# Attention and a top-2 mixture of experts on one core: another order of the slots by hand

## The chip, the cores and the metric

The program runs on one core of one Trainium2 chip. The metric is the time of one execution on the device in microseconds. Five runs of the kernel before gave 513.17, 511.36, 506.5, 507.58 and 507.99 us: a median of 507.99 (506.5 to 513.17).

## The reference

Blockwise causal attention (8 batches, 8 heads, 576 positions, head size 64, blocks of 64) is followed by a router that picks two of eight experts for each of the 4608 tokens, and by the experts themselves, two layers each.

```python
scores = scale * np.matmul(q, k.transpose(0, 1, 3, 2))
mask = block_i >= block_j
scores = np.where(mask, scores, -1000000000.0)
attn = np.exp(scores - max); attn = attn / attn.sum
x = np.matmul(attn, v)            # as (4608, 512): heads side by side
...
logits = x @ w_gate
noise_scale = np.log1p(np.exp(x @ w_noise))
noisy_logits = logits + noise_scale * noise
top2 = np.argpartition(-noisy_logits, 2, axis=1)[:, :2]
top2_w = softmax over the two
for e in range(E):
    h = np.maximum(x[mask] @ w1[e], 0.0)
    out[mask] += top2_w[mask, k, None] * (h @ w2[e])
```

## The kernel before, in words

**Attention.** The eight batches are worked in four groups of two batches (`NG = 4`). q and k of a group come in five chunks (0 to 4) through a ring of eight raw buffers each (`load_qk`, line 200), on GpSimd's queue. `transpose_qk` turns a chunk on TensorE (L250; the half chunks "4A" and "4B" on L252) into a PSUM tile of a pool with two buffers, and copies it into `qT` or `kT`: q on VectorE (L255), k on ScalarE (L262), k of chunk 1 on VectorE (L260); after chunk 0 a small VectorE copy (L265) follows. Both lie in one tile, `hq`, that the experts use again later. Chunk c holds blocks 16c to 16c+15 of a group's heads, so head h needs blocks 9h to 9h+8.

A group is 26 units (`UG`): two sets of four heads, three pieces of scores a head and one unit for the last block. A unit is TensorE matmuls (L292, L303) into one of two PSUM tiles `sc`, and one exp on ScalarE (L295, L306) into `esc`; the last unit of a set also zeroes parts of `esc` on VectorE (L309). `av_tile` multiplies `esc` by v (L333, L344) into one of two PSUM buffers "av" and normalises on VectorE (reciprocal L348, multiply L349) into the rows `xr`; the first tile of a group also zeroes the tail of `xr` (L322). v is loaded by `load_v` (L207) into one of two tiles, one for even and one for odd groups.

**Router.** `x_transpose` (L363, copy L364 on VectorE) turns a group's rows, and the generator `router` does the rest in 16 steps: steps 0 to 2 are the logits matmuls (L376) with their activations (L380 to L382), step 8 is two matmuls that count rows per expert (L420, L421), and the others are VectorE work on small tiles; the last sets `slots`. Then `scatter` (L484) writes 36 row tiles per pair of groups into `xd[half]` by indirect DMAs from GpSimd's queue, 18 a group; each also waits for the last but one pacing activation (`pace[-2]`). Groups 0 and 1 make half 0, groups 2 and 3 half 1.

**Experts.** Sixteen blocks (`SEQ`: experts 0, 1, 2 of half 0, the same of half 1, then in turn) each do `layer1` (L559, activation L562) and `layer2` (L571); layer 1's first part of the next block stands ahead of layer 2. `load_x` (L504) loads a block's rows by a transposing DMA from SyncE's queue, once all 36 scatters of its half have landed; `load_rec` (L511) loads the rows' records under the same condition, and `read_rec` turns them into row numbers and weights. Layer 2 writes `ysb` (four buffers, L576), stored by SyncE (L577); for a token's second expert the first one's rows are gathered (L598), added (L580) and the output row is written (L582), both indirect DMAs on GpSimd's queue. In block order, the load of block 3's x (expert 0 of half 1) stands behind the stores of block 1 and `load_rec(1)` on SyncE's queue. `load_w` (L227) loads weights on GpSimd's queue in four parts per expert: experts 0 and 1 into a pool `wE` with two buffers of its own, expert 2 into `wM`, which lies where the raw chunks of q and k lay and is opened, with the x tiles, after the last of these are turned.

**What sets the order.** Nothing is scheduled by a program: each engine runs its instructions in the order in which they are written. After each score unit u, `run(u)` issues what was put into slot u by `at(slot, fn, ...)`, in the order in which it was put there. Slots 0 to 103 are the attention units, 104 and 105 stand alone, and from 106 on each slot follows one step (`layer1` or `layer2` tile) of the experts. A queue runs its DMAs in the order of issue, and a DMA on GpSimd's or SyncE's queue also waits for the one eight places before it on that queue.

Of the kernel before, what the change touches and what calls it, by code (L numbers as in the profile page):

```python
# [19 lines left out]
def kernel(  # L20
# [23 lines left out]
    TG = 9  # L44
# [19 lines left out]
    UG = 2 * UN  # L64
# [32 lines left out]
    wE = main.enter_context(tc.tile_pool(name="wE", bufs=2))  # L97
# [112 lines left out]
    def v_loads(g):  # L210
        return [(load_v, g, idx) + r for idx in range(TG) for r in token_rows(g, idx)]
# [257 lines left out]

    RSTEPS = 16  # L470
    rgen = {}

    def router_step(g):
        if g not in rgen:
            rgen[g] = router(g)
        next(rgen[g])

    scat = [[] for _ in range(NH)]
    zfill = [[] for _ in range(NH)]
# [134 lines left out]
    todo = {}  # L614

    def at(slot, fn, *args):
        todo.setdefault(slot, []).append((fn, args))

    def run(slot):
        for fn, args in todo.pop(slot, ()):  # L620
            fn(*args)

    def after(ins, slot):
# [75 lines left out]
    for g in range(NG):  # L699
        s0 = g * UG  # L700
        last = g == NG - 1

        for nm, ch, i in (("q", 1, 0), ("k", 1, 3), ("k", 2, 5), ("q", 2, 7), ("k", "4A", 8), ("q", "4A", 9),
                          ("q", 3, 15), ("k", 3, 16)):
            at(s0 + i, transpose_qk, g, nm, ch)
        if not last:
            for nm, ch, i in (("q", 0, 14), ("k", 0, 17), ("q", "4B", 24), ("k", "4B", 24)):
                at(s0 + i, transpose_qk, g + 1, nm, ch)
            for i, (fn, *a) in enumerate(v_loads(g + 1)):
                at(s0 + 10 + i, fn, *a)  # L710
            at(s0 + 18, load_qk, g + 1, (2,))
            at(s0 + 20, load_qk, g + 1, (3,))
        if g + 2 < NG:
            for i, ch in ((21, 4), (22, 0), (24, 1)):
                at(s0 + i, load_qk, g + 2, (ch,))
        for i, a in enumerate((16, 16, 17, 18, 19, 19, 20, 21)):
            at(s0 + a, av_tile, g, 0, i)
        for i in range(2):
            at(s0 + 22 + i, av_tile, g, 0, 8, i)
        r0 = s0 + UG  # L720
        if not last:
            avs = (1, 2, 2, 4, 5, 5, 6, 7, 9, 10)
            xts_ = (6, 8, 11, 11, 12)
        if g < 2:
            rsl = (13, 13, 14, 17, 18, 19, 20, 21, 23, 24, 25, 26, 27, 28, 30, 31)
            r1 = 31
        elif g == 2:
            rsl = (13, 13, 14, 16, 17, 17, 18, 19, 21, 22, 22, 23, 23, 24, 24, 25)
            r1 = 26
        else:  # L730
            avs, xts_ = (0, 0, 1, 1, 2, 2, 3, 3, 4, 4), range(2, 7)
            rsl = (7, 7, 7, 8, 9, 9, 10, 11, 12, 13, 13, 14, 14, 15, 15, 16)
            r1 = 16
        for i in range(8):
            at(r0 + avs[i], av_tile, g, 1, i)
        for i in range(2):
            at(r0 + avs[8 + i], av_tile, g, 1, 8, i)
        for j in range(5):
            at(r0 + xts_[j], x_transpose, g, j)
        for j in range(RSTEPS):  # L740
            at(r0 + rsl[j], router_step, g)
        for j in range(2 * TG):
            at(r0 + r1 + (4 * j // 5 if last else j), scatter, g, j)
    at(4, setup_consts)
    at(3, sort_nz, 0)
    at(5, transpose_nz, 0)
    at(5, spread_nz, 0, 0)
    at(7, spread_nz, 0, 1)
    at(9, sort_nz, 1)
    at(12, transpose_nz, 1)  # L750
    at(12, spread_nz, 1, 0)
    at(13, spread_nz, 1, 1)
    at(UG + 4, clear_x, 0, UG + 3)
    at(2 * UG + 4, clear_x, 1, 2 * UG + 3)
    for k in range(4):
        at(2 * UG + k, load_w, wE, 0, k)
        at(3 * UG + 7 + 2 * k, load_w, wE, 1, k)
    for u in range(NG * UG):
        score_unit(*divmod(u, UG))
        run(u)  # L760
        if u == 3 * UG + 19:
            raws_up.close()
            ffn["x"] = raws_up.enter_context(tc.tile_pool(name="xgp", bufs=3, side="right", reuse_waits="tile"))
            wM = raws_up.enter_context(tc.tile_pool(name="wM", bufs=1, side="right", reuse_waits="tile"))
            at(3 * UG + 25, load_x, 0)
            at(3 * UG + 25, load_x, 1)
            at(4 * UG, load_rec, 0)
            at(4 * UG + 3, load_x, 2)
            for k in range(4):
                at(4 * UG + 1 + 4 * k, load_w, wM, 2, k)  # L770

    slot = NG * UG
    at(slot + 6, read_rec, 0)
# [8 lines left out]
    for i in range(2):  # L782
        run(slot)
        slot += 1
# [122 lines left out]
```

## Time and profile before

| | value |
|---|---|
| median of five runs | 507.99 us |
| the profiled execution | 513.18 us, span 511.3 us |
| PE busy (matmul) | 430.7 us, 84% |
| PEld busy (weight load) | 262.0 us, 51% |
| ACT busy | 255.6 us, 50% |
| POOL busy | 255.1 us, 50% |
| DVE busy | 164.0 us, 32% |
| mean granted TensorE clock | 0.91 |
| DMA moved | 78.68 MB, mean 154 GB/s |

PE is TensorE, DVE is VectorE, ACT is ScalarE, POOL is GpSimd, SP is SyncE with its DMA queue (SPq). A busy share is an average over stages with different limits. Where a row names a wait, "A <- B" says that A stood idle until B. The profiled execution is the slowest of the runs shown: 5.2 us above their median.

### The profile page before, as it was taken

What the parts mean: (1) busy time and instruction counts of PE and PEld (TensorE: products, weight loads), DVE (VectorE), ACT (ScalarE), POOL (GpSimd) and SP (SyncE); (2) the same over time, 40 slices, a digit from 0 to 9 for tenths busy, and PEclk for the clock granted to TensorE, in tenths of its full rate; (3) what the DMA queues carried; (4) which work ended last, traced back from release to release, by engine and by line L of the source; (5) the groups of instructions that cost most, each with busy time, mean ns of one, the idle gap of its engine ahead of it and who ended that gap; (6) DMA issues with size and microseconds to landing.
All of it is one profiled execution on the core that took longest, in us unless ns stands there. A gap on an engine that the chain in (4) does not pass through costs nothing.

```text
span 511.3 us, 9896 instructions
## 1 busy us (share of the span) xinstructions
PE 430.7 (84%) x3936; PEld 262.0 (51%) x3952; DVE 164.0 (32%) x532; ACT 255.6 (50%) x339; POOL 255.1 (50%) x301
## 2 busy tenths in 40 slices
PE   3879988789787698971894999999889999997993
PEld 2446755556454474530452555655555665564561
DVE  1646757546845768000030001011011112112212
ACT  2869877557756423521352445544534554553330
POOL 8776283378476266575030113344526465555533
PEclk9999976776976699995797999999999999999998
DMA  9999899889677599543679467979998998995212
GB/s 143 152 145 170 165 159 207 206 95 115 119 152 163 133 162 196 146 142 98 75 155 152 117 135 159 192 149 189 130 236 219 150 242 225 154 201 169 84 65 92
DMA packets 134826, 78.68 MB, mean 154 GB/s; under 512 B 96193, under 2 KB 124611, under 8 KB 134772
## 3 DMA queue, kind: packets, MB, share of 16 engines
q0 software_dynamic: 70560, 55.79, 69.8%
q1 hardware_dynamic: 64212, 22.18, 22.0%
q8 instruction: 33, 0.54, 0.4%
q14 instruction: 21, 0.17, 0.1%
HBM read 68.28 MB, written 33.13 MB: 198 GB/s over the span
## 4 chain that ended last, share of the span: by engine, by line
PE 54%; DVE 11%; issue 10%; DMA 10%; POOL 7%; ACT 4%; another core or an unknown queue 3%; POOLq 0%; SPq 0%; DVEq 0%; ACTq 0%
PE yp L571 20%; PE hp L559 18%; DMA xg<-xd 4%; PE sc L292 4%; PE av L333 4%; PE tp L250 2%; DMA yg<-yd,orow 2%; PE av L344 2%; PE tp L363 2%; DVE xr L349 2%; POOL out_dram L582 2%; DMA vt<-in_v_dram 2%; DVE hq L255 1%; POOL yg L598 1%
## 5 line engine op out<-in xcount | busy, mean ns | idle before, releaser
L559 PE MATMUL hp<-xg,w1sb 128*128 128x320 bf16 x960 | 137.1, 303 | 25.1 <-ACT hq L562 16.0
L571 PE MATMUL yp<-w2sb,hq 128*128 128x512 bf16 x624 | 141.8, 381 | 7.9 <-DVE yo L580 4.9
L559 PEld LDWEIGHTS <-w1sb 128*128 128x128 bf16 x1024 | 100.9, 99 | 69.2 <-issue 18.0
L562 ACT ACTIVATE hq<-hp 128x640 bf16<-128x640 f32 x128 | 89.4, 703 | 84.7 <-PE hp L559 75.6
L580 DVE SCALAR_TENSOR_TENSOR yo<-yp,wrow,yg 128x512 f32<-128x512 f32 x46 | 34.5, 751 | 260.6 <-ACT ysb L576 178.1
L295 ACT ACTIVATE esc<-sc 128x1024 bf16<-128x1024 f32 x96 | 96.2, 1023 | 41.1 <-PE sc L292 30.0
L571 PEld LDWEIGHTS <-hq 128*128 128x128 bf16 x640 | 63.0, 98 | 82.7 <-issue 13.0
L484 POOL DMA_INDIRECT xd<-xr,slots x72 | 71.4, 992 | 58.9 <-DVE rden L348 18.3
L576 ACT ACTIVATE ysb<-yp,wrow 128x512 bf16<-128x512 f32 x70 | 48.1, 687 | 97.1 <-PE yp L571 72.1
L598 POOL DMA_INDIRECT yg<-yd,orow x46 | 47.1, 1025 | 88.3 <-ACT hq L562 65.0
L582 POOL DMA_INDIRECT out_dram<-yo,trow x46 | 45.9, 999 | 77.1 <-DVE yo L580 67.8
L292 PE MATMUL sc<-hq 64*128 64x512 bf16 (+4 forms) x320 | 50.2, 367 | 12.6 <-DVE xr L322 3.9
L333 PE MATMUL av<-vt,esc 128*128 128x65 bf16 x640 | 37.0, 218 | 10.2 <-DVE xr L349 6.4
L207 POOL DMA_DIRECT2D vt<-in_v_dram x40 | 34.3, 879 | 14.5 <-PE av L344 10.1
L333 PEld LDWEIGHTS <-esc 128*128 128x128 bf16 x640 | 29.4, 113 | 23.4 <-DVE xr L349 9.4
L250 PE MATMUL tp<-ident,t 128*64 128x128 bf16 x512 | 27.7, 268 | 5.3 <-DMA t<-in_q_dram 4.3
L349 DVE TENSOR_TENSOR xr<-av,rden 128x256 bf16<-128x256 f32 x72 | 30.6, 424 | 2.7
L250 PEld LDWEIGHTS <-t 128*64 128x64 bf16 x512 | 21.0, 138 | 13.8 <-issue 6.9
L292 PEld LDWEIGHTS <-hq 64*128 64x128 bf16 x320 | 12.8, 100 | 25.0 <-issue 5.8
L348 DVE RECIPROCAL rden<-av 128x4 f32<-128x4 f32 x72 | 13.5, 187 | 31.4 <-PE av L333 12.3
L262 ACT ACTIVATE hq<-tp 128x1024 bf16<-128x1024 bf16 (+1 forms) x20 | 17.0, 849 | 11.3 <-PE tp L250 5.2
L255 DVE COPY hq<-tp 128x1024 bf16<-128x1024 bf16 (+1 forms) x24 | 14.4, 601 | 20.8 <-PE tp L250 12.6
(125 smaller groups left out, 247.7 us busy)
## 6 DMA issues: line engine op xcount, KB each, us to landing
yd<-ysb SPq DMA_DIRECT2D x70, 128.0 KB
w1sb<-in_moe_w_dram POOLq DMA_DIRECT2D x16, 512.0 KB
w2sb<-in_moe_w_dram POOLq DMA_DIRECT2D x16, 512.0 KB
t<-in_q_dram POOLq DMA_DIRECT2D x16, 256.0 KB
t<-in_k_dram POOLq DMA_DIRECT2D x16, 256.0 KB
vt<-in_v_dram POOLq DMA_DIRECT2D x32, 128.0 KB
xd<-zero SPq DMA_DIRECT2D x16, 132.0 KB
xd<-xr,slots POOLq DMA_INDIRECT x72
```

The source lines that it names most:

```text
L250: nc.tensor.transpose(to[64 * hf:64 * hf + 64, :, r, :], raw[:, hf, r * 64:(r + 1) * 64], ident)
L292: nc.tensor.matmul(out=sc[:, hf, off:off + z - a], lhsT=kT[sl, c0 + jt * P:c0 + jt * P + P], rhs=qT[sl, c0 + a:c0 + z], start=True, stop=True)
L295: ins = nc.scalar.activation(out=esc[:, hh, :, piece * 512:(piece + 1) * 512], in_=sc, func=AF.Exp, scale=scale)
L333: nc.tensor.matmul(out=av[:, hh, :], lhsT=esc[:, hh, hf, c:c + P], rhs=vb[:, 4 * hf + jt, h, :], start=(jt == 0), stop=(jt == ib))
L349: nc.vector.tensor_tensor(out=xr[:, idx, st * SET * D:(st + 1) * SET * D].rearrange("p (h d) -> p h d", h=SET), in0=av[:, :, 0:D], in1=rde ...
L484: ins = nc.gpsimd.indirect_dma_start(out=xd[half].bitcast(I32), out_offset=bass.IndirectOffsetOnAxis(ap=slots[:, g * TG + idx, i:i + 1], a ...
L559: nc.tensor.matmul(out=hp[:, n, 0:NW], lhsT=w1sb[:, db, fb * P:(fb + 1) * P], rhs=xgs[b][:, db, n * NW:(n + 1) * NW], start=(db == 0), sto ...
L562: ins = nc.scalar.activation(out=hs[b][:, fb, :].rearrange("p (n w) -> p n w", n=2), in_=hp[:, :, 0:NW], func=AF.Relu)
L571: nc.tensor.matmul(out=yp, lhsT=hs[b][:, fb, c * P:(c + 1) * P], rhs=w2sb[:, fb, :], start=(fb == 0), stop=(fb == FB - 1))
L576: nc.scalar.activation(out=ysb, in_=yp, func=AF.Copy, scale=w)
L582: ins = nc.gpsimd.indirect_dma_start(out=out, out_offset=bass.IndirectOffsetOnAxis(ap=trow[half][:, e, c:c + 1], axis=0), in_=yo, in_offse ...
L598: ins = nc.gpsimd.indirect_dma_start(out=yg, out_offset=None, in_=yd[half][0:e * CAP, :], in_offset=bass.IndirectOffsetOnAxis(ap=orows[hal ...
```

## The change

The functions stay the same; what changes is the slot in which each is issued, and the order within a slot. Within a slot, `run` now sorts what is left by `rank`: router steps that have only VectorE work first, then AV tiles, then transposes (of q, k and of rows), then the router steps with matmuls (0, 1, 2, 8), then all else. Copies of q and k come up to five slots sooner (chunk 3), in group 0 the next group's chunk 0 five slots later; v and the row chunks 2 and 3 of the next group are loaded one to five slots sooner. AV of the second set begins in the next group's slot 0 instead of 1, row transposes and router steps follow two to five slots sooner, and so do the scatters. The weights of experts 0 and 1 are loaded at slots 46 to 49 and 72 to 75 instead of 52 to 55 and 85 to 91, those of expert 2 at 100 to 109 instead of 105 to 117; the x loads of blocks 0 to 2 and the records come three to six slots sooner. The row transposes and the AV tiles of the last group keep their slots.

```diff
     def run(slot):
-        for fn, args in todo.pop(slot, ()):
+        def rank(item):
+            fn, args = item
+            if fn is router_step:
+                return 3 if rgen_n.get(args[0], 0) in (0, 1, 2, 8) else 0
+            return {av_tile: 1, transpose_qk: 2, x_transpose: 2}.get(fn, 4)
+        items = todo.pop(slot, [])
+        while items:
+            items.sort(key=rank)
+            fn, args = items.pop(0)
             fn(*args)
...
-        for nm, ch, i in (("q", 1, 0), ("k", 1, 3), ("k", 2, 5), ("q", 2, 7), ("k", "4A", 8), ("q", "4A", 9),
-                          ("q", 3, 15), ("k", 3, 16)):
+        for nm, ch, i in (("q", 1, 0), ("k", 1, 2), ("k", 2, 4), ("q", 2, 6), ("k", "4A", 7), ("q", "4A", 8),
+                          ("q", 3, 10), ("k", 3, 12)):
             at(s0 + i, transpose_qk, g, nm, ch)
         if not last:
-            for nm, ch, i in (("q", 0, 14), ("k", 0, 17), ("q", "4B", 24), ("k", "4B", 24)):
+            for nm, ch, i in (("q", 0, 14 if g else 19), ("k", 0, 17 if g else 22), ("q", "4B", 22), ("k", "4B", 21)):
                 at(s0 + i, transpose_qk, g + 1, nm, ch)
             for i, (fn, *a) in enumerate(v_loads(g + 1)):
-                at(s0 + 10 + i, fn, *a)
-            at(s0 + 18, load_qk, g + 1, (2,))
-            at(s0 + 20, load_qk, g + 1, (3,))
+                at(s0 + 9 + i, fn, *a)
+            at(s0 + 13, load_qk, g + 1, (2,))
+            at(s0 + 16, load_qk, g + 1, (3,))
...
-        for i, a in enumerate((16, 16, 17, 18, 19, 19, 20, 21)):
-            at(s0 + a, av_tile, g, 0, i)
-        for i in range(2):
-            at(s0 + 22 + i, av_tile, g, 0, 8, i)
+        for i, a in enumerate((15, 16, 17, 18, 18, 19, 20, 21, 22, 23)):
+            at(s0 + a, av_tile, g, 0, *((i,) if i < 8 else (8, i - 8)))
         r0 = s0 + UG
         if not last:
-            avs = (1, 2, 2, 4, 5, 5, 6, 7, 9, 10)
-            xts_ = (6, 8, 11, 11, 12)
+            avs = (0, 1, 1, 3, 4, 4, 5, 6, 7, 8)
+            xts_ = (3, 5, 7, 9, 10)
         if g < 2:
-            rsl = (13, 13, 14, 17, 18, 19, 20, 21, 23, 24, 25, 26, 27, 28, 30, 31)
-            r1 = 31
+            rsl = (11, 11, 12, 13, 14, 15, 16, 17, 19, 20, 21, 22, 23, 24, 25, 26)
+            r1 = 26
         elif g == 2:
-            rsl = (13, 13, 14, 16, 17, 17, 18, 19, 21, 22, 22, 23, 23, 24, 24, 25)
-            r1 = 26
+            rsl = (11, 11, 12, 13, 13, 14, 15, 16, 18, 19, 19, 20, 20, 21, 22, 22)
+            r1 = 23
         else:
             avs, xts_ = (0, 0, 1, 1, 2, 2, 3, 3, 4, 4), range(2, 7)
-            rsl = (7, 7, 7, 8, 9, 9, 10, 11, 12, 13, 13, 14, 14, 15, 15, 16)
-            r1 = 16
+            rsl = (6, 6, 7, 8, 8, 9, 9, 10, 11, 12, 12, 12, 13, 13, 13, 14)
+            r1 = 14
...
         for j in range(2 * TG):
-            at(r0 + r1 + (4 * j // 5 if last else j), scatter, g, j)
+            at(r0 + r1 + (j if g < 2 else 4 * j // 5), scatter, g, j)
...
     for k in range(4):
-        at(2 * UG + k, load_w, wE, 0, k)
-        at(3 * UG + 7 + 2 * k, load_w, wE, 1, k)
+        at(2 * UG - 6 + k, load_w, wE, 0, k)
+        at(2 * UG + 20 + k, load_w, wE, 1, k)
...
-        if u == 3 * UG + 19:
+        if u == 3 * UG + 13:
...
-            at(3 * UG + 25, load_x, 0)
-            at(3 * UG + 25, load_x, 1)
-            at(4 * UG, load_rec, 0)
-            at(4 * UG + 3, load_x, 2)
+            at(3 * UG + 19, load_x, 0)
+            at(3 * UG + 20, load_x, 1)
+            at(3 * UG + 21, load_rec, 0)
+            at(4 * UG, load_x, 2)
             for k in range(4):
-                at(4 * UG + 1 + 4 * k, load_w, wM, 2, k)
+                at(3 * UG + 22 + 3 * k, load_w, wM, 2, k)
```

Outside this cut the noise steps of group 0 (sort, transpose and spread of the router's noise) move by one to three slots, and a counter of router steps (`rgen_n`) is added for the ranks.

More of the change, by code (lines that the diff above doesn't have):

```diff
@@ L471 @@
     rgen = {}
+    rgen_n = {}
     def router_step(g):
@@ L476, in router_step @@
         next(rgen[g])
+        rgen_n[g] = rgen_n.get(g, 0) + 1
     scat = [[] for _ in range(NH)]
@@ L708 @@
                 at(s0 + i, transpose_qk, g + 1, nm, ch)
             for i, (fn, *a) in enumerate(v_loads(g + 1)):
-                at(s0 + 10 + i, fn, *a)
-            at(s0 + 18, load_qk, g + 1, (2,))
-            at(s0 + 20, load_qk, g + 1, (3,))
+                at(s0 + 9 + i, fn, *a)
+            at(s0 + 13, load_qk, g + 1, (2,))
+            at(s0 + 16, load_qk, g + 1, (3,))
         if g + 2 < NG:
-            for i, ch in ((21, 4), (22, 0), (24, 1)):
+            for i, ch in ((20, 4), (22, 0), (24, 1)):
@@ L733 @@
-            r1 = 16
[L734 to L737, printed above, removed]
+            rsl = (6, 6, 7, 8, 8, 9, 9, 10, 11, 12, 12, 12, 13, 13, 13, 14)
+            r1 = 14
+        for i in range(TG + 1):
+            at(r0 + avs[i], av_tile, g, 1, *((i,) if i < 8 else (8, i - 8)))
         for j in range(5):
@@ L742 @@
         for j in range(2 * TG):
-            at(r0 + r1 + (4 * j // 5 if last else j), scatter, g, j)
[L744 to L752, printed above, removed]
+            at(r0 + r1 + (j if g < 2 else 4 * j // 5), scatter, g, j)
+    at(3, setup_consts)
+    at(4, sort_nz, 0)
+    at(8, transpose_nz, 0)
+    at(8, spread_nz, 0, 0)
+    at(9, spread_nz, 0, 1)
+    at(10, sort_nz, 1)
+    at(14, transpose_nz, 1)
+    at(14, spread_nz, 1, 0)
+    at(15, spread_nz, 1, 1)
     at(UG + 4, clear_x, 0, UG + 3)
```

## The prediction

> **What bounds the kernel now.** I read the page's chain of waits first (PE 54%, DVE 11%, DMA 10%, no engine over 84% busy), then the busy times by stage, cut where the score units of each group begin and where the chain changes. The columns are stretch, length, busy time (and count) of PE, PEld, DVE, ACT and POOL, granted TensorE clock, DMA share and GB/s.
>
> ```profile
> ...
> 12.00:47.80 35.80, 29.37 (x390) 18.53 (x392) 20.13 (x107) 28.40 (x32) 25.93 (x35) 1.00 2.32 153
> 47.80:82.50 34.70, 31.40 (x569) 21.33 (x565) 23.80 (x70) 28.61 (x35) 20.05 (x27) 0.88 1.41 172
> 82.50:127.10 44.60, 37.89 (x547) 24.51 (x548) 26.05 (x89) 28.08 (x33) 25.39 (x27) 0.67 0.94 149
> 127.10:173.60 46.50, 35.10 (x546) 22.85 (x546) 29.89 (x101) 29.69 (x36) 25.66 (x28) 0.77 0.64 131
> ...
> 196.70:250.60 53.90, 35.86 (x200) 20.17 (x200) 8.21 (x30) 17.98 (x27) 31.16 (x32) 0.87 0.61 137
> ...
> 276.20:505.00 228.80, 218.82 (x1275) 126.22 (x1288) 32.85 (x49) 104.87 (x151) 99.58 (x102) 0.99 0.78 163
> ```
>
> The first four rows are the four attention groups. PE is nearest to full, yet idle 6.4, 3.3, 6.7 and 11.4 us (length less busy), and the same work costs it 31.4 us at clock 0.88 but 37.9 at 0.67. The last row is the expert stage: PE 96% busy, nothing of the change reaches it. Between them (196.70 to 250.60) PE idles 18 us. Why, the POOL timeline, the SP timeline and the chain in order of time say (start us, duration, what, and in brackets the idle time before it):
>
> ```profile
> 208.86 0.98 POOL L484 DMA_INDIRECT xd<-xr,slots  x1 [0.30 <-issue]
> 213.43 1.05 POOL L598 DMA_INDIRECT yg<-yd,orow  x1 [3.58 <-issue]
> 214.78 1.01 POOL L484 DMA_INDIRECT xd<-xr,slots  x1 [0.31 <-issue]
> ...
> 236.63 0.98 POOL L484 DMA_INDIRECT xd<-xr,slots  x1 [0.30 <-issue]
> ```
> ```profile
> 239.22 0.32 SPq L577 DMA_DIRECT2D yd<-ysb  x1
> 240.60 0.38 SPq L511 DMA_DIRECT2D rc<-xd  x1
> 241.09 5.11 SPq L504 DMA_TRANSPOSE xg<-xd  x1
> ```
> ```profile
> 241.09 9.50 DMA xg<-xd
> 250.59 0.05 issue
> 250.63 1.47 PE hp L559 x8
> ```
>
> The rows of half 1 must all be scattered before block 3 (expert 0, half 1) can load its x: last scatter at 236.63, load at 241.09, landed at 250.6, and from there the program runs to 511.3 whatever came before. Without this PE would ask for block 3 earlier: 14 us of idle (13.0 before 241.44, 1.1 before 211.63) stand before it. So block 3's x is the gate, and what ends earlier in attention or in the scatters moves the end one for one, up to some 14 us of the scatters' own gain. Last, what PE waits for up to 240 (total, times, longest):
>
> ```profile
> PE av L333 <- DVE xr L349: 6.4, 11, 2.1
> ...
> PE tp L250 <- DMA t<-in_q_dram: 4.3, 2, 2.3
> PE sc L292 <- DVE xr L322: 3.9, 3, 1.7
> ...
> PE sc L292 <- ACT hq L262: 3.0, 6, 1.1
> PE av L333 <- DVE esc L309: 2.7, 1, 2.7
> PE sc L292 <- issue: 2.4, 4, 1.5
> ```
>
> The scores (sc) stand behind the copies of q and k out of PSUM. "DVE xr L322" is the small memset right behind the copy of q chunk 3, whose score is the very next unit.
>
> **The change part by part.**
>
> Copies sooner. The sc waits to go: 3.9 (q chunk 3, slot 15 to 10), 1.9 of the 3.0 on ACT (1.1 is the first score at 11.4 us and stays), 1.0 and 0.9 on the DVE copies of k and q chunk (smaller rows of the same view), and 1.5 of "issue" at 160.07, right behind the copy of k chunk 3 on ACT: 9.2 us. The cover is two slots of 1.67 us (173.6 us over 104 slots), 3.3 us, against a transpose of 1.07 and a copy of 0.69 to 1.23. In group 0, chunk 0 of group 1 moves from slot 14 to 19, past its landing (PE waited 2.29 at 30.27): 2.3 us. Together 11.5. ACT and DVE work is the same, 28 to 30 us of ACT per group, so a part comes back as waits for exp. Bounds 0 and -11.5; I take -8, nearer the rows, since ACT has 6 us or more idle in each of groups 1 to 3.
>
> Clock. Groups 2 and 3 pay 6.5 and 3.7 us more PE time than group 1. The drops stand near idle: clock 1.00 in the group with the shortest waits per matmul, 0.67 where the 1.7 us waits are. If both reached group 1, -10.2; if groups 1 and 3 fell to group 2's rate, +9.3. I take -3, a third of the gain, because only the sc part of their idle goes. [...]
>
> AV sooner and first in its slot. AV of a second half set now begins in the slot in which its last exp runs, and needs the DVE memset of esc. The one place that shows this order is the last group: 2.66 us (row "DVE esc L309"). Three groups get it new: 0 to +8. In groups 0 and 1 the memset began at 46.40 and 82.31, before the next unit's scores were over (47.3, 83.1), so I take +2.
>
> Router steps ahead of AV. The same DVE instructions in another order. They end at slot r0+22 instead of 25 (group 2) and r0+14 instead of 16 (group 3), where r0 is 26 slots after the group's first. Two costs: AV's normalisation (0.18 + 0.42) waits behind a step of 0.5 to 1.3 us, with two PSUM buffers as cover; I take 0 here and price the rest as a rival.
>
> Scatters. Group 2's 18 begin at slot 101, not 104, four in five slots; POOL then has them done before group 3's router ends (205.5 on the old clock; the DVE chain from 195.4 is back to back and keeps its place). Group 3's first, at 207.58 behind group 2's, can start at 205.8, and four instead of two stand ahead of the gather, which waits for block 0's stores. If the gather stays at 213.43, fourteen scatters and one output row remain at 1.28 us: the last starts at 214.78 + 14 x 1.28 = 232.7, against 236.63: -3.9. If the stores land sooner because expert 2's weights (slots 100 to 109, not 105 to 117) are through, the gather follows at 210.9 and it is -6.4. If SP is still held by the fifth store of block 1 (239.22, tied with the scatters), it is 0. I take -4.
>
> Weights of experts 0 and 1 at slots 46 to 49 and 72 to 75 (52 to 55 and 85 to 91). On POOL's queue the first four now stand among the loads of q and k of group 3: 4 x 0.7 us of issue and 2 MB (512 KB each by the page's issue rows), 13.7 us at 153 GB/s. Those loads are needed 16 slots (27 us) later, so 0; without that cover, up to 13.7 us. Expert 1's no longer sit between the scatters of group 1: 4 x 1.1 us of POOL, not on the path. x of blocks 0 and 1 and the records are asked for on SP five or six slots sooner, for use at 178.65; now issued at 172.09 and 174.79: 0. The noise steps of group 0 move by one to three slots: 0.
>
> Sum: -8 - 3 + 2 - 4 = -13. The profiled execution spans 511.3 us (513.18 with what lies around it) and is the slowest of the runs; I carry the difference over to their median, 507.99: 495.
>
> **Rivals.**
> A. Nothing much: attention is limited by ACT and DVE together, so copy waits come back as exp waits, and SP's store gate leaves the scatters worth nothing. For it: ACT's 28 to 30 us and DVE's 24 to 30 us of a group; the tie at 239. Against: group 1 shows 34.7 us with the same work as groups that take 45. It leaves the 2.3 us of the DMA wait: 505.
> B. Slower: DVE order. Per group eight slots hold both AV and a router step; if the two AV buffers don't cover, each costs a step, some 0.8 us: 3 groups x 8 x 0.8 = 19. Against the -12 of copies and scatters this is +7: 515. It decides once a step plus normalisation (0.6) is longer than PE's next tile and score (0.7 to 1.1 + 0.4). For it: the 6.4 us that AV already waits on DVE xr; against: DVE is idle 35% of group 3.
> C. Larger: the copies' idle was what dropped the clock; groups 2 and 3 come down to group 1's 34.7 us (-21.7), and -4 from the scatters: 482.
> That the change doesn't do what it says is excluded for the order: each engine's queue differs as described.
>
> **How the numbers follow.** Forecast 0.60 at 495, its own range 486 to 503 (copies -11.5 to -5, scatters -6.4 to 0, clock -6 to 0); A 0.20 (502 to 509); B 0.12 (512 to 522); C 0.08 (476 to 487). The range 484 to 509 leaves out B and half of C. What tells from no change is 1%, 5 us: faster (below 502.9) is nearly all of the forecast, C and a little of A, 0.69; same 0.20; slower 0.11.
>
> **What would show it.** Copies: the sc rows on L322, L262 and the copies of L255 and L260 sum to under 4 us, not 9. Clock: above 0.75 in groups 2 and 3. Scatters: group 3's last starts some 59 us after the last exp of attention, not 63.3 (236.63 less 173.3). Gate: x of block 3 lands 10 to 15 us before 250.6, and from there to the end stays 260.7. It is wrong if AV waits on DVE xr grow past 15 us (B), or if the groups keep 35, 35, 45 and 46 us (A).

## The result, and the profile after

| | before | after |
|---|---|---|
| median, the runs beside each other | 511.25 us (79 runs) | 508.33 us (42 runs) |
| ratio after to before, 95% interval | | 0.9957 (0.9937 to 0.9977) |
| the profiled execution | 513.18 us, span 511.3 | 503.92 us, span 502.1 |
| start of the first exp of groups 0 to 3, and of the last exp (ACT timeline) | 12.0, 47.8, 83.2, 129.2, 173.2 | 12.1, 41.6, 73.6, 114.7, 164.8 |
| last scatter of half 1 | 236.63 | 229.12 |

The change takes 0.4% off, some 2 to 3 us, where 13 were forecast. The two profiles flatter it: before's lies 2 us above its median, after's 4 us below. Medians here are over all runs and ratios over the undisturbed ones alone, so that the two can differ.

The busy times by stage of the changed kernel, columns as before (stretch, length, busy time and count of PE, PEld, DVE, ACT, POOL, clock, DMA share, GB/s):

```profile
12.00:41.60 29.60, 25.41 (x390) 16.55 (x388) 20.00 (x107) 27.34 (x31) 21.94 (x28) 0.83 2.08 148
41.60:73.60 32.00, 29.17 (x570) 20.35 (x567) 26.07 (x82) 28.55 (x36) 21.16 (x30) 0.95 1.66 199
73.60:114.70 41.10, 32.75 (x571) 22.31 (x571) 28.05 (x93) 28.52 (x35) 27.80 (x30) 0.86 1.07 186
114.70:164.80 50.10, 37.91 (x526) 24.00 (x525) 27.96 (x98) 27.34 (x33) 26.94 (x31) 0.67 0.81 148
...
264.30:502.00 237.70, 220.44 (x1275) 126.64 (x1288) 32.93 (x49) 104.96 (x151) 100.62 (x103) 0.97 0.77 159
```

Groups 0 to 2 are 6, 3 and 5 us shorter, but group 3 takes 50.1 us, where before took 44.0 from first to last exp (the 46.5 of the prediction's row begin 2.1 us ahead of its first exp), and PE idles 12.2 of them at clock 0.67. What PE waits for up to 240 us (total, times, longest):

```profile
PE sc L292 <- ACT esc L295: 10.8, 13, 2.8
...
PE av L333 <- DVE xr L349: 6.7, 8, 2.0
...
PE tp L250 <- issue: 3.8, 7, 1.0
...
PE av L344 <- issue: 2.7, 4, 1.1
...
PE sc L292 <- ACT hq L262: 1.1, 1, 1.1
```

The wait of scores for the copy of chunk 3 (xr L322) is gone, and of the ACT copies only the first score's 1.1 us is left: that step did what was forecast. In its place stand 10.8 us of waits for an exp to free its PSUM (1.4 us before), and waits that no engine explains ("issue"). Scatters of group 3 and output rows on GpSimd, and SyncE's queue:

```profile
199.81 0.98 POOL L486 DMA_INDIRECT xd<-xr,slots  x1 [6.62 <-DVE xr L466]
...
216.64 0.97 POOL L486 DMA_INDIRECT xd<-xr,slots  x1 [2.87 <-ACT hq L564]
...
222.71 0.98 POOL L584 DMA_INDIRECT out_dram<-yo,trow  x1 [2.53 <-DVE yo L582]
...
229.12 0.98 POOL L486 DMA_INDIRECT xd<-xr,slots  x1 [0.31 <-issue]
```
```profile
231.86 0.38 SPq L513 DMA_DIRECT2D rc<-xd  x1
232.34 5.44 SPq L506 DMA_TRANSPOSE xg<-xd  x1
```

The first scatter waits for the router (6.62 us of idle GpSimd), the last starts 64.3 us after the last exp (63.4 before). All that the gate gained, it gained in attention: block 3's x is asked for at 232.34, not 241.09.

Where group 3 loses its time shows in the timeline of PE (start, duration, operation, count, and in brackets the idle time before), and of POOL beside it:

```profile
139.49 0.30 PE L250 MATMUL tp<-ident,t 128*64 128x128 bf16 x3
140.12 0.28 PE L250 MATMUL tp<-ident,t 128*64 128x128 bf16 x3 [0.33 <-issue]
140.86 0.24 PE L250 MATMUL tp<-ident,t 128*64 128x128 bf16 x1 [0.46 <-issue]
141.59 0.43 PE L250 MATMUL tp<-ident,t 128*64 128x128 bf16 x4 [0.48 <-issue]
143.01 0.44 PE L250 MATMUL tp<-ident,t 128*64 128x128 bf16 x4 [1.00 <-issue]
144.44 0.27 PE L250 MATMUL tp<-ident,t 128*64 128x128 bf16 x1 [0.98 <-issue]
```
```profile
139.84 0.98 POOL L486 DMA_INDIRECT xd<-xr,slots  x1 [0.30 <-issue]
141.12 0.98 POOL L486 DMA_INDIRECT xd<-xr,slots  x1 [0.31 <-issue]
142.41 0.98 POOL L486 DMA_INDIRECT xd<-xr,slots  x1 [0.30 <-issue]
143.69 0.97 POOL L486 DMA_INDIRECT xd<-xr,slots  x1 [0.31 <-issue]
```

One tile of sixteen transposes, 0.6 to 1.1 us elsewhere, takes 5.2 us here: PE does a few, stops, and does a few more, with every operand on hand, while GpSimd issues row scatters 1.28 us apart, one right behind the other. I call such a row of scatters a train. Theory H, to be tested: the copies do bring their gain, and the changed kernel gives part of it back because its trains are longer; the weights of expert 1, which stood among the scatters of group 1, are now ahead of them. Rival theory A is the forecast's own: attention is limited by exp, and the copies' waits come back as waits for it.

### The profile page after: what moved, and what is told of

Same layout as the page of the kernel before. It is cut to its first block, busy times and chain, and to the rows that moved or that the text cites. A ratio compares the mean times of both kernels' runs of the same rounds, so it can differ in the third digit from the quotient of the medians.

```text
span 502.1 us, 9904 instructions
## 1 busy us (share of the span) xinstructions
PE 427.1 (85%) x3936; PEld 259.8 (52%) x3952; DVE 164.4 (33%) x532; ACT 253.0 (50%) x339; POOL 254.7 (51%) x301
## 5 line engine op out<-in xcount | busy, mean ns | idle before, releaser
L561 PE MATMUL hp<-xg,w1sb 128*128 128x320 bf16 x960 | 139.2, 305 | 17.4 <-DMA xg<-xd 8.9
L561 PEld LDWEIGHTS <-w1sb 128*128 128x128 bf16 x1024 | 101.8, 100 | 63.5 <-issue 10.4
L295 ACT ACTIVATE esc<-sc 128x1024 bf16<-128x1024 f32 x96 | 94.7, 1026 | 27.7 <-PE sc L292 15.3
L573 PEld LDWEIGHTS <-hq 128*128 128x128 bf16 x640 | 63.4, 99 | 76.5 <-issue 7.4
L600 POOL DMA_INDIRECT yg<-yd,orow x46 | 47.1, 1025 | 81.7 <-ACT hq L564 63.5
L292 PE MATMUL sc<-hq 64*128 64x512 bf16 (+4 forms) x320 | 44.6, 349 | 12.4 <-ACT esc L295 10.8
L333 PE MATMUL av<-vt,esc 128*128 128x65 bf16 x640 | 36.6, 215 | 9.8 <-DVE xr L349 6.7
L333 PEld LDWEIGHTS <-esc 128*128 128x128 bf16 x640 | 28.7, 111 | 26.3 <-DVE xr L349 12.2
L348 DVE RECIPROCAL rden<-av 128x4 f32<-128x4 f32 x72 | 13.3, 185 | 22.5 <-PE av L333 10.5
```

The lines of the kernel that those rows point to most:

```text
L292: nc.tensor.matmul(out=sc[:, hf, off:off + z - a], lhsT=kT[sl, c0 + jt * P:c0 + jt * P + P], rhs=qT[sl, c0 + a:c0 + z], start=True, stop=True)
L295: ins = nc.scalar.activation(out=esc[:, hh, :, piece * 512:(piece + 1) * 512], in_=sc, func=AF.Exp, scale=scale)
L333: nc.tensor.matmul(out=av[:, hh, :], lhsT=esc[:, hh, hf, c:c + P], rhs=vb[:, 4 * hf + jt, h, :], start=(jt == 0), stop=(jt == ib))
L561: nc.tensor.matmul(out=hp[:, n, 0:NW], lhsT=w1sb[:, db, fb * P:(fb + 1) * P], rhs=xgs[b][:, db, n * NW:(n + 1) * NW], start=(db == 0), sto ...
L573: nc.tensor.matmul(out=yp, lhsT=hs[b][:, fb, c * P:(c + 1) * P], rhs=w2sb[:, fb, :], start=(fb == 0), stop=(fb == FB - 1))
L600: ins = nc.gpsimd.indirect_dma_start(out=yg, out_offset=None, in_=yd[half][0:e * CAP, :], in_offset=bass.IndirectOffsetOnAxis(ap=orows[hal ...
```

## The experiments

Kernels of one group below ran on the same chip, beside runs of the kernel before there; the five groups ran on five chips. "Gaps" are idle times of PE of 0.3 us or more that no engine explains ("issue" or "remote"), counted in the timeline up to 240 us.

**First chip (before 506.07 us).** The copies alone, in the kernel before:

```diff
-("q", 1, 0), ("k", 1, 3), ("k", 2, 5), ("q", 2, 7), ("k", "4A", 8), ("q", "4A", 9), ("q", 3, 15), ("k", 3, 16)
+("q", 1, 0), ("k", 1, 2), ("k", 2, 4), ("q", 2, 6), ("k", "4A", 7), ("q", "4A", 8), ("q", 3, 10), ("k", 3, 12)
-("q", 0, 14), ("k", 0, 17), ("q", "4B", 24), ("k", "4B", 24)
+("q", 0, 14 if g else 19), ("k", 0, 17 if g else 22), ("q", "4B", 22), ("k", "4B", 21)
```

> The kernel before with only the new slots of the copies (transposes of q and k) in it; AV, router, scatters, weights and rows loads stay as they were. Theory H (the copies do bring their 8 to 11 us, and the changed kernel gives most of it back because its row scatters now follow one another at 1.28 us in longer trains, under which TensorE crawls): the trains are those of before, so most of the gain is there: 4 to 8 us below before (503 to 507 where before has 511). Theory A (attention is limited by exp and its PSUM buffers: what waited for a copy now waits for an exp): 0 to 2 us below before (509 to 511). The waits of sc on DVE xr L322 are gone under both.

Measured: 506.11 us, ratio 0.9938 (0.9886 to 0.9990). The interval takes in figures of both theories. In the profile the groups take 31.4, 35.7, 41.7 and 46.2 us, the last exp is at 167.1, and the waits of scores for exp grow to 6.8 us.

The weights of experts 0 and 1 back at their old slots, all else as in the change:

```diff
-        at(2 * UG - 6 + k, load_w, wE, 0, k)
-        at(2 * UG + 20 + k, load_w, wE, 1, k)
+        at(2 * UG + k, load_w, wE, 0, k)
+        at(3 * UG + 7 + 2 * k, load_w, wE, 1, k)
```

> The changed kernel with the weights of experts 0 and 1 at their old slots (52 to 55, and 85, 87, 89, 91), so that those of expert 1 again stand among the scatters of group 1. Theory H: the trains of group 1's scatters are broken up again, and the last attention group loses less: 3 to 5 us below the changed kernel (503 to 505 where it has 508). Theory A: the weights are hidden work in both places: within 1 us of the changed kernel. A third reading, that the earlier weights help the loads of group 3: 1 to 3 us slower than the changed kernel.

Measured: 504.03 us, ratio to before 0.9933 (0.9887 to 0.9979); group 3 takes 44.8 us, not 50. By the time the step is not resolved against the change's 0.9957. Group 3 alone is as H has it, but group 2 takes 42.8 us, more than in any profile of the changed kernel (38.4 to 41.2), and the last exp is at 162.8, amid that kernel's 160.3 to 165.4. What group 3 wins, group 2 loses, and attention as a whole is not shorter.

Scatters of groups 0 and 1 held apart by dummy work on GpSimd:

```diff
+        if g < 2:
+            for _ in range(4):
+                nc.gpsimd.memset(junk, 0.0)     # junk: [P, 96] F32
         ins = nc.gpsimd.indirect_dma_start(
```

> The changed kernel with four small memsets on GpSimd (some 1 us of its time) ahead of each scatter of groups 0 and 1, so that scatters begin 2.2 us apart or more instead of 1.28; 36 x 1 us more work on GpSimd, all else as it is. Theory H: TensorE no longer crawls in groups 1 to 3; attention ends 4 to 8 us sooner, of which the end sees most: 500 to 505 where the changed kernel has 508. Theory A: no gain, 508, or up to 5 us slower, because loads of v, q and k behind the scatters on GpSimd's queue come later.

Measured: 532.85 us, ratio 1.0489 (1.0424 to 1.0554): no theory's figure. Its profile holds two answers. Attention is as H has it: not one gap, groups 2 and 3 take 36.5 and 41.9 us (41.1 and 50.1 in the changed kernel), and the last exp is at 153.4, 11.4 us sooner:

```profile
75.00:111.50 36.50, 30.70 (x570) 21.29 (x570) 27.48 (x92) 28.46 (x36) 25.49 (x69) 0.91 0.77 154
111.50:153.40 41.90, 33.60 (x521) 22.40 (x522) 28.28 (x99) 27.17 (x32) 32.27 (x73) 0.71 0.93 134
```

The memsets do two things at once, though: they hold the scatters apart, and they push some of them out of attention. Twelve start in group 2 and twelve in group 3, where the first profile of the changed kernel has 17 and 20, so this run does not tell wider from fewer.

And 36 scatters 2.5 us apart are not out in time: PE then stands 40.5 us for the x of block 0:

```profile
PE hp L565 <- DMA xa<-xd: 40.5, 1, 40.5
```

The changed kernel without the sorting of a slot's steps (`items.sort(key=rank)` left out):

> The changed kernel without the sorting of a slot's steps (router steps ahead of AV, AV ahead of the transposes), so that they run in the order in which they are entered. Theory H: the order within a slot does not matter: within 2 us of the changed kernel (506 to 510). Rival B (AV's normalisation stands behind router steps on VectorE, and that ate the gain): 4 us or more below the changed kernel, and the waits of av on DVE xr fall from 6.7 us to under 4.

Measured: 509.5 us, ratio 1.0050 (1.0006 to 1.0093), and the waits of av for xr are 13.3 us, not under 4. Rival B falls: putting router steps first did not cost AV its time, since without it nothing is faster. Whether the sorting is worth nothing or up to 1% is not shown, because the changed kernel was not run on this chip (elsewhere it has 0.9957 to 1.0039).

**Second chip (before 508.03 us).** One memset ahead of each scatter of groups 0 and 1 instead of four:

> The changed kernel with one small memset (0.31 us) ahead of each scatter of groups 0 and 1, not four: trains at 1.6 us instead of 1.28, 11 us more work on GpSimd, and the last of half 0's rows still out before block 0 wants them (some 12 us of room in the changed kernel). Theory H (trains slow TensorE): attention ends 3 to 8 us sooner than the 164.8 of the changed kernel's profile, gaps of issue in its trains are rarer, and with x on time the end follows: 501 to 506 where the changed kernel has 508. If 1.6 us is still too dense, or if the four memsets helped for another reason: no change, 507 to 510, and the gaps stay.

Measured: 502.24 us at the median, ratio 0.9984 (0.9926 to 1.0042). Seventeen gaps of 7.7 us in all, most of them in trains, and group 3 takes 49.8 us. But the scatters are not 1.6 us apart: the memset falls in part into the 0.3 us that GpSimd stood idle between two scatters anyway, and they begin every 1.34 us instead of 1.28:

```profile
138.28 0.98 POOL L489 DMA_INDIRECT xd<-xr,slots  x1 [0.17 <-issue]
139.25 0.20 POOL L488 MEMSET junk<- 128x96 f32 x1
139.62 0.98 POOL L489 DMA_INDIRECT xd<-xr,slots  x1 [0.17 <-issue]
```

So this run hardly tests the spacing. Its time is another matter: 502.24 lies where H has it, 4.1 us below the changed kernel on the same chip (506.38, below), although gaps stay and attention ends later (163.5 against 160.5). Gaps and time do not go together here, and what the one memset brought is open.

The change with the copies at their old slots (the first diff above, turned round):

> The changed kernel with the old slots of the copies (transposes of q and k), everything else as in the change. If the copies alone are what the change brings (the copies alone measured 0.6% under before, the whole change 0.4%): 1 to 4 us slower than the changed kernel, so the same as before or slower by up to 1%; the waits of sc on DVE xr L322 are back at some 4 us. If the other parts bring something of their own (the forecast had +2 - 4 for AV and scatters): 1 to 4 us below before.

Measured: 517.01 us, ratio 1.0232 (1.0144 to 1.0320), 10.6 us above the changed kernel on the same chip (506.38, below). Neither expectation has that. The waits of scores for copies (total, times, longest):

```profile
PE sc L292 <- DVE hq L255: 7.1, 7, 1.9
...
PE sc L292 <- DVE hq L260: 5.6, 4, 2.4
PE sc L292 <- ACT hq L262: 5.2, 6, 1.1
```

Scores wait 17.9 us for these three. The likely reason, that AV and router work now stands in front of the late copies on VectorE, is shown only in part: ahead of four of the eight copies that scores waited for after 60 us, VectorE had stood idle for 0.8 to 1.0 us. In any case the copies and the rest do not add: the copies take 2.3 to 3.2 us off alone, and some 10 with the rest in place, which without them costs 2.3%.

The weights spread among the scatters instead of in two lumps:

```diff
-        at(2 * UG - 6 + k, load_w, wE, 0, k)
-        at(2 * UG + 20 + k, load_w, wE, 1, k)
+        at(2 * UG + 1 + 2 * k, load_w, wE, 0, k)
+        at(3 * UG + 2 + 3 * k, load_w, wE, 1, k)
```

> The changed kernel with the weights of experts 0 and 1 spread singly among the scatters of groups 0 and 1 (slots 53, 55, 57, 59 and 80, 83, 86, 89; two pieces of 256 KB to 512 KB at the first of each), so that GpSimd's queue itself breaks up the trains with work that has to be done anyway. Theory H: fewer gaps of issue, 2 to 6 us below the changed kernel (502 to 506 where it has 508). If trains do not matter or the weights' bytes hold up the scatters behind them instead: 508 or up to 4 us slower.

Measured: 499.13 us, ratio 0.9897 (0.9845 to 0.9949), below the 502 to 506 of H. Group 3 falls to 42.8 us, and the last exp is at 155.1:

```profile
73.60:112.30 38.70, 33.28 (x573) 22.82 (x574) 27.99 (x94) 28.56 (x36) 29.77 (x32) 0.85 1.19 201
112.30:155.10 42.80, 35.16 (x525) 22.36 (x524) 27.79 (x97) 27.29 (x33) 26.52 (x30) 0.74 0.96 171
```

Gaps are not gone: seven, of 2.8 us in all.

The changed kernel again:

> The changed kernel once more, unedited, for a second profile and for its time on the same chip as the others: every theory says 506 to 510, 0 to 1% below before. The first profile was at the lower end of its runs (503.9 where the median was 508.3); if groups 2 and 3 vary by several us from one execution to the next, their lengths differ from 41 and 50 here.

Measured: 506.38 us, ratio 1.0034 (0.9973 to 1.0094). Group 3 takes 49.6 us, as in the first profile, so its length is no accident of one execution. But it loses them in another form. PE idles 17.9 us there, and only 2.6 of these are gaps; the longest waits are the following, while GpSimd issues eleven scatters from 136.02 to 149.82, all 1.28 us apart:

```profile
147.44 0.18 DVE L348 RECIPROCAL rden<-av 128x4 f32<-128x4 f32 x1 [6.38 <-remote]
148.14 0.40 PE L333 MATMUL av<-vt,esc 128*128 128x65 bf16 x4 [5.96 <-DVE xr L349]
...
151.82 0.18 DVE L348 RECIPROCAL rden<-av 128x4 f32<-128x4 f32 x1 [3.74 <-remote]
152.52 0.30 PE L420 MATMUL pp<-ms,ones_mat 128*128 128x144 bf16 x1 [3.98 <-DVE xr L349]
```

PE waits for an AV tile to be normalised, and VectorE, which is idle and not busy with the router, waits for a signal whose sender the trace does not name ("remote"; a matmul whose record is missing would look the same). The fifth chip's profile of the changed kernel has the same pair, 7.23 and 2.34 us. So a count of PE's gaps misses part of the stall. Such idle times of VectorE, 1 us or more between 70 and 180 us (on the first chip 3.80 us ahead of 160.41 in before and 2.32 ahead of 130.75 in after), stand in every profile that has gaps, and in none that has not.

**Third chip (before 493.73 us).** Two profiles of the kernel before, its copies with spread weights, and spread weights with memsets in the changed kernel:

> The kernel before, unedited, for a second profile. Its first profile was at 513.2 us, above the median of its runs; if that profile is typical in attention, the last exp is again at 170 to 176 us and the rest takes 338; if it was a long one, the last exp is at 163 to 168 and the changed kernel's gain in attention (160.5 and 164.8 in two profiles) is some 4 us, not 8 to 13.

> The kernel before, unedited, for a third profile: as the one ahead of it. Two of three profiles with the last exp above 170 would leave the loss of the gain to the expert stage, two below 168 to the first profile having been a long one.

Measured: 495.88 and 498.31 us, with the last exp at 158.4 and 158.2. Both expectations asked about the execution and the answer was the chip: its runs of before have a median 12 to 18 us below those on the other chips, not one gap stands in either profile, and groups 2 and 3 take 37.6 and 36.6 us (first of the two):

```profile
84.20:121.80 37.60, 32.88 (x573) 22.12 (x574) 26.96 (x92) 29.08 (x35) 23.87 (x25) 0.84 1.03 165
121.80:158.40 36.60, 30.00 (x521) 20.31 (x520) 27.77 (x94) 27.20 (x33) 27.41 (x29) 0.86 0.84 167
```

The same scatters run there in trains at 1.28 us; PE does not stall. So the stall goes with trains on some chips: four of the five in these experiments show it. Each chip was visited once, so that chip and visit cannot be told apart. The stall is in the kernel before too, and there groups 2 and 3 together take some 15 us more than here. PE is idle for 5 to 8 of them; for the other 6 to 10 it is busy, at a lower granted clock (0.69 to 0.81 in these groups, 0.83 to 0.91 here). Whether the stalls lower the clock or it is lower there for a reason of its own, no run separates.

```diff
-        at(2 * UG + k, load_w, wE, 0, k)
-        at(3 * UG + 7 + 2 * k, load_w, wE, 1, k)
+        at(2 * UG + 6 + 2 * k, load_w, wE, 0, k)
+        at(3 * UG + 6 + 2 * k, load_w, wE, 1, k)
```

This edit and the new copy slots, in the kernel before:

> The kernel before with the new slots of the copies, and with the weights of experts 0 and 1 among the scatters of groups 0 and 1 (slots 58, 60, 62, 64 and 84, 86, 88, 90); AV, router, scatters and rows loads as before. If what the spread weights won (1.0% under before, with the change's other parts in) rests on breaking the trains alone: 0.6 to 1.2% under before. If it needs the change's earlier scatters: no better than the copies alone, 0 to 0.6% under before.

Measured: 487.99 us, ratio 0.9898 (0.9862 to 0.9933), last exp at 152.1, no gaps. On this chip there are no stalls to break, so that this gain does not come from broken trains. How much of it the copies bring alone was not measured here.

Spread weights in the changed kernel, with two memsets before each of the first ten scatters of group 0 and one before each of group 1:

> The changed kernel with the weights spread singly among the scatters, and besides two small memsets ahead of each of the first ten scatters of group 0 and one ahead of each of group 1: 12 us more on GpSimd, half 0's rows out at about 156 instead of 143.9. Theory H: attention ends at 150 to 155 (155.1 without the memsets), and the end is 0 to 4 us below that of the kernel without them (499): 495 to 499. If the spread weights had broken the trains already, or the rows are late then: 499 to 504.

Measured: 500.12 us, ratio 1.0119 (1.0053 to 1.0184). H's condition was absent: no kernel has gaps here. Attention ends at 148.4, 10 us before that of the kernel before, and the program ends later, since the rows of half 0 are late:

```profile
PE hp L564 <- DMA xa<-xd: 20.2, 1, 20.2
PE hp L564 <- DMA xg<-xd: 15.0, 2, 9.2
```

So attention time was worth something here only as far as GpSimd's queue kept up.

**Fourth chip (before 508.55 us).** Four kernels again:

> The changed kernel again, on whichever chip comes. Theory H, as it now stands (trains of scatters slow TensorE, but not on every chip: on the one where two profiles of before show no gap of issue at all, before took 494 and its groups 2 and 3 took 37 and 36 us, not 46 and 44): where the profiles show no gaps, the changed kernel's attention is about 10 us shorter than before's 158 and the end 6 to 12 us below before; where they show gaps, 0 to 1% below before. If the trains are not the cause: the same 0 to 1% on both kinds of chip.

Measured: 508.89 us, ratio 1.0039 (0.9990 to 1.0088), with gaps; group 3 takes 50.3 us.

> The new slots of the copies alone, in the kernel before, again. Theory H: without gaps in the profiles 5 to 8 us below before; with gaps 2 to 5 us below. If the copies' gain is lost elsewhere: 0 to 3 us below on either.

Measured: 504.09 us, ratio 0.9954 (0.9908 to 0.9999), with gaps; last exp at 162.3, group 3 takes 46.2 us.

> The new slots of the copies, and the weights of experts 0 and 1 among the scatters, in the kernel before, again: 0.6 to 1.4% below before on either kind of chip (1.0% measured on the one without gaps); with gaps in the profiles at least as far below as the copies alone.

Measured: 503.0 us at the median of six, ratio 0.9892 (0.9772 to 1.0012); three gaps, group 3 takes 45.8 us.

> The changed kernel with the weights spread singly among the scatters, again: 1.0% below before measured on a chip with gaps. Theory H: where the profiles show gaps it beats the changed kernel by 0.5 to 1.5%; where they show none, breaking the trains is worth nothing and it is within 0.4% of the changed kernel. If the weights' place matters for another reason (the loads behind them): the same distance on both kinds of chip.

Measured: 506.18 us, ratio 0.9966 (0.9919 to 1.0013): 0.7% under the changed kernel beside it, as H has it where there are gaps; six gaps of 2.3 us are left. Attention again ends at 155.2. The rival reading, that the weights' place matters for another reason than trains, was to be told by this pair on a chip without gaps, and there it was not run.

On this chip the copies alone are ahead of the whole change by 4.8 us of median.

**Fifth chip (before 506.94 us).** One profile of before, and the changed kernel:

> The kernel before, unedited, for one more profile beside the changed kernel on one chip. Theory H: if its profile shows gaps of issue in the trains, groups 2 and 3 take 42 to 47 us each and the last exp is at 168 to 175 (the changed kernel's were at 160.5 to 165.4 on such chips, three profiles); if it shows none, 36 to 38 each and the last exp at about 158.

> The changed kernel on the same chip. Theory H: without gaps, groups 2 and 3 take 36 to 39 us each, the last exp is at 146 to 150 and the end 6 to 12 us below before; with gaps, group 3 takes 49 to 51 us as in all three profiles so far, the last exp is at 160 to 166, and the end is 0 to 3 us below before. If group 3's 50 us come from the schedule and not from the trains, it takes 49 to 51 us on either kind of chip.

Measured: before 514.44 us with the last exp at 171.8 and groups 2 and 3 at 44.1 and 44.3; after 506.04 us (six runs, no ratio), last exp at 160.3, group 3 at 48.8. Both show gaps, so the chip gave a second profile of before with stalls, and not the changed kernel without them; that was never seen.

| profiles on chips with gaps | groups 0 to 3, us | last exp |
|---|---|---|
| before (first, fifth) | 35.8, 35.4, 46.1, 44.0; 36.5, 34.9, 44.1, 44.3 | 173.2; 171.8 |
| after (four) | 29.5, 32.0, 41.2, 50.0; 29.1, 31.8, 38.4, 49.6; 29.6, 33.3, 40.2, 50.3; 28.1, 32.1, 39.5, 48.8 | 164.8; 160.5; 165.4; 160.3 |
| copies alone (two) | 31.4, 35.7, 41.7, 46.2; 30.7, 32.6, 40.5, 46.2 | 167.1; 162.3 |
| after, weights spread (two) | 29.5, 31.8, 38.7, 42.8; 29.5, 32.0, 38.0, 43.5 | 155.1; 155.2 |
| after, weights at old slots | 29.8, 33.1, 42.8, 44.8 | 162.8 |
| after, one memset | 29.5, 32.2, 39.6, 49.8 | 163.5 |
| after, four memsets (no gap) | 29.6, 33.3, 36.5, 42.0 | 153.4 |
| third chip, without gaps: before (two) | 36.2, 36.0, 37.6, 36.5; 36.3, 35.1, 38.4, 36.4 | 158.4; 158.2 |
| third chip: before, copies and spread weights | 31.3, 33.0, 38.5, 37.3 | 152.1 |
| third chip: after, spread weights and memsets | 29.7, 33.1, 37.2, 36.1 | 148.4 |

## Why the prediction was wrong

The forecast was 495, with -13 us; measured are -2.9 us of median and, on the chips of the experiments, -1.7, +0.3 and -0.9. Three steps failed: the weights' move, put at nothing, which costs; the scatters, which bring nothing; and the size of the copies' gain. Besides, the forecast started from 507.99, the median of five runs, where that of 79 is 511.25. In the first profile attention is 8.4 us shorter, close to the -9 of copies, clock and AV together; that is luck, as it is made up of -14.5 in groups 0 to 2 and +6 in group 3. By steps:

**Copies, -8.** The mechanism was right: the waits named there are gone, and the group 0 wait of 2.3 us with them. The size was not. Alone the copies measure -0.6 and -0.5%, 2 to 3 us, and in the two profiles part of the waits stands at exp again (6.8 and 7.2 us, 1.4 before), which is what rival A said. In company they are worth some 10, since the other parts make late copies dearer; how, is shown only in part.

**Weights of experts 0 and 1 sooner, 0.** This is the step that failed most plainly. The prediction saw that expert 1's weights "no longer sit between the scatters of group 1" and dismissed it as GpSimd time off the path. They were the spacing of those scatters. With the weights in front, group 3 takes 49 to 50 us in four profiles of four; spread, 42.8 and 43.5. In time, the spread weights are 1.4% and 0.7% below the changed kernel on the two chips where both ran (0.9897 to 1.0034, 0.9966 to 1.0039). On the second of these the copies alone are 0.8% below the whole change, so the rest of the change costs time there, and spreading the weights wins most of it back. That the weights' place matters is thus shown. That the old slots would do is not: with them group 3 takes 44.8, but group 2 grows and attention is no shorter. Nor is it shown that the stall is the whole of it, since gaps stay when the weights are spread, and since in the lumped form scatters of group 1 also stand behind the weights' landing (idle GpSimd of 1.81 and 1.54 us ahead of those at 131.49 and 134.00), and bunch up behind it.

**Scatters, -4.** Wrong: 0. From the last exp to the last scatter it was 63.4 and 63.5 us before, and 64.3, 63.7, 62.7 and 64.0 after. The step had group 2's scatters as what held group 3's back; in the changed kernel GpSimd stands idle 6.62 us for the router and starts 35.0 us after the last exp (34.4 before). And the 18 us it gave to the rest left out two waits, 2.87 for a pacing activation and 2.53 for an output row.

**Clock, -3.** Group 2 went from 0.67 to 0.86, group 3 from 0.77 to 0.67, so half of what was to be shown came about. The reading was also too simple: group 0 did the same matmuls in 29.37 us at clock 1.00 and in 25.41 at 0.83, so busy time is not the clock's alone. Nor do the drops stand near idle throughout. The changed kernel's rows lean that way, with 0.67 where PE idles 12.2 of 50.1 us and 0.95 where it idles 2.8 of 32.0; but before's group 0 idles 6.4 of 35.8 us at 1.00 and its group 1 3.3 of 34.7 at 0.88, and between 80 and 90 us of before PE was busy 9.20 of 10 us at 0.54. The place of the transposes does not tell the changed kernel's groups 1 and 3 apart: both have them in the same slots, at 0.95 and 0.67. No run shows what lowers the clock, so that the -3 was the author's estimate.

**AV sooner, +2, and router before AV, 0.** The wait for the memset of esc is 0.5 us, where before had 2.7, so the +2 did not come. What the order within a slot is worth stays open (1.0050 without it; 0.9957, 1.0034 and 1.0039 with it, each on another chip). Rival B is out: AV's waits for xr are 6.7 to 12.3 us in the four profiles, under its 15, and in the two longest (6.0 and 6.2 us) VectorE stood idle.

**Gate, 260.7 us fixed.** Right for the first profile: 262.3 from block 3's first matmul at 239.83 to the end. Not fixed otherwise: from asking for block 3's x to the end it is 270.2 and 273.7 us before, and 269.8, 278.3, 287.8 and 270.2 after. The longest of these (the changed kernel on the fourth chip) shows where, in PE's timeline and in that of ACT:

```profile
430.11 9.51 PE L561 MATMUL hp<-xg,w1sb 128*128 128x320 bf16 x48 [8.19 <-ACT hq L564]
```
```profile
428.78 0.69 ACT L578 ACTIVATE ysb<-yp,wrow 128x512 bf16<-128x512 f32 x1 [10.03 <-DMA yd<-ysb]
429.37 1.29 ACT L564 ACTIVATE hq<-hp 128x640 bf16<-128x640 f32 x2
```

PE stands 8.19 us in layer 1 of a late block, for the activation of 429.37. On ScalarE that one stands behind a copy into `ysb`, and the copy stands 10.03 us for a store on SyncE's queue that has to free one of the four buffers. So a late store holds up ScalarE, and through it TensorE. Such waits of PE for that activation come to 0.7, 6.8, 13.3 and 1.2 us in the four profiles of after, and 1.9 and 6.3 in the two of before; the same chain stands ahead of 5.8 of the 6.8 and 3.1 of the 6.3. They are not the change's, but as large as what it was to bring.

**What is left open.** In the profiles with gaps, block 3's x is asked for at 241.1 and 238.9 before and at 232.3, 227.2, 231.3 and 227.4 after: 10.4 us sooner in the mean, close to the forecast. The expert stage gives 4.6 of that back in the mean (272.0 to 276.5 us; the spread within a kernel is as large). The rest is missing between the profiles and the unprofiled runs: all four profiles of before lie 2 to 8 us above their medians, those of after on both sides. Whether before's unprofiled runs have the shorter attention can't be seen. So what ate the gain is shown in part: 5 to 7 us in group 3 against spread weights, scatters that brought nothing, and an expert stage that waits for stores and scatters the end by more than the gain.

**A version that looks better than both.** The copies' new slots and spread weights in the kernel before: 0.9898 (0.9862 to 0.9933) on the third chip, and on the fourth, where before and after stood at 508.6 and 508.9, a median of 503.0, though with an interval that reaches 1.0012 (six runs), and not told apart from the copies alone (504.09). The change with spread weights had 0.9897 (0.9845 to 0.9949) and 0.9966 (0.9919 to 1.0013).

## What to carry to other kernels

A queue's order is not only a matter of what is late on it: what stands between two DMAs also sets how close together they come (here scatters 1.28 us apart with nothing between them, 2.5 with four memsets), so price a moved load by the neighbours it leaves, too. Before adding up the parts of a reordering, ask which parts put work in front of which: here one part was worth 3 us alone and 10 beside the others. And a gain ahead of a gate is worth what the stages behind it let through (here 10.4 us in the mean ahead of the gate, of which the expert stage gave 4.6 back): look in them for a second limit, and in more than one profile.

## What the runs showed of the hardware

On four chips of five, TensorE stalls in trains of indirect row scatters 1.28 us apart: its instructions come in small batches with 0.3 to 1.1 us between them, although operands and buffers are there. Before has 4 and 5 gaps up to 240 us (2.8 and 1.9 us; 1.5 of the 2.8 are the wait of 160.07, which the prediction rightly put down to a copy), after 12, 7, 13 and 7 (7.9, 5.1, 6.8 and 4.1 us); most of them stand in trains, and the groups lengthen by more than the gaps. Two more things go with them on these chips: idle times of VectorE that end with no named sender, up to 7.23 us, and in the kernel before a lower granted clock (0.69 to 0.81 in groups 2 and 3, 0.83 to 0.91 on the third chip). A low clock stands without gaps, too: 0.71 in group 3 with four memsets, 0.78 in group 3 of the third chip's copies with spread weights. At 1.34 us apart the gaps stay (17); at 2.5 us and more there are none, but then fewer scatters lie in attention, too. On the third chip none of four kernels shows one, with trains of eight and nine scatters in the kernel before. What makes it so, the profiles don't show: the DMA share is 0.29 in the stretch of 139.5 to 144.7 us shown above, against 2.08 in group 0, and ACT, DVE and POOL instructions keep their durations: an exp of 1024 columns takes 1.02 us and AV's multiply 0.42 in groups 1 and 3 alike, and the scatters of that stretch 0.97 to 0.98 us, as those from 199.81 on.

Chips differ by more than this change: the kernel before has a median of 493.7 us on one, and 506 to 511 us on the others, each visited once.
